# Zero products beside thin matmuls, signs ahead of a sigmoid, and weight loads placed around the decays

## The chip, the cores and the metric

The kernel runs on one core of a Trainium2 chip. The metric is the device time of one execution in microseconds. TensorE is called PE (its weight loads PEld), VectorE DVE, ScalarE ACT, GpSimd POOL, and SyncE, which issues nearly all DMAs, SP.

## The reference

Two things one after the other: a recurrent attention (mLSTM) with exponential gates over 768 steps, for 4 batches and 8 heads of 40, and a bilinear feed-forward on its output, 3072 rows of 320.

```
m_new = max(f + m, i);  f_stab = exp(f + m - m_new);  i_stab = exp(i - m_new)
C = f_stab * C + i_stab * outer(v, k);   n = f_stab * n + i_stab * k
y = sigmoid(o) * (C q) / max(|n q|, 1)
out = ((x @ w_a) * (x @ w_b)) @ w_out        # x is y as rows, 320 -> 1536 -> 320
```

The weights come as float64; the other inputs as float32.

## The kernel before

**Tiling.** The sequence is cut into 6 pieces of 128 steps, and with 4 batches that makes 24 chunks, n = 0 to 23 (piece n // 4, batch n % 4). Inside a chunk the recurrence is a masked, decay-weighted attention; between pieces a state of 40 x 42 per head is carried. Chunks are gathered into 9 moe blocks of 2 or 3 chunks (`sizes`), and `moe_block` multiplies a block's rows with the weights, each value split in a high and a low part.

**Stages of a chunk**, by letter: E builds the decay matrix, A transposes q and k, B makes the scores and weighs them with E, C multiplies with the values, U updates the state, F divides and gates, D transposes the result into the rows of its moe block. Chunks 0 to 5 (`NF32` = 6) take the float32 forms `begin_a`, `begin_b`, `begin_i`, `begin_c`. Chunks 0 to 3 (`NE` = 4) build E on PE (`begin_e`); from chunk 4 on `stage_e` reads the decays back from DRAM, broadcast to all partitions (`load_g`, tile `gbc`, two buffers, freed by the value products of the chunk two before), masks them on POOL (L483) and takes eight exponentials on ACT (L490). `gates_rest` computes these decays on DVE and stores them to `g_dram` (L289).

**Weights.** They come as 32 stages (0 to 31). `fetch(to)` issues the DMAs of all stages below `to` that are not yet issued, on SP. A stage is converted from the words of its float64 in steps: `signs` (ACT, L412), `words` (three DVE instructions, L423 to L426), `leading` (ACT copy, L439), `rests` (two products on PE, L449 and L450, and an addition on DVE, L457, or two halved ones, L455). An up product of the first moe block waits, through `need`, until its stages are converted. The raw tiles of stages 26 to 31 use the room in which q, k and v of chunks 2 and 3 lie.

**Order.** The opening, `start()`, runs inside `in_order()`: every engine gets its instructions in the written order, SP's DMAs too. So does what is left of `gates_rest` behind it. After that the order is the scheduler's: it starts from the order of tracing, by a modelled timeline, and `tc.issue_after(x)` adds that what is traced in its block is queued behind x on x's engine. `attention()` traces the stages of chunk after chunk, with later letters for the next chunk, in between the pieces of the moe blocks.

`busy(count)` issues `count` matmuls of zeros (L959, 336 columns) into a bank that nobody reads; `dense` puts three such ahead of some products of chunks 2 and 3. `weigh` (POOL, L585) scales the values for U with one buffer; `gate_o` is the sigmoid of the output gates (ACT, L217), and the first one in the opening carries a load of ACT's tables.

Of the kernel before, what the change touches and what calls it, by code (L numbers as in the profile page):

```python
# [8 lines left out]
F32 = mybir.dt.float32  # L9
# [5 lines left out]
AF = mybir.ActivationFunctionType  # L15
# [5 lines left out]
def kernel(  # L21
# [13 lines left out]
    nc = tc.nc  # L35
    B, H, S, D = q.shape
    DM, DFF = w_a.shape
    P = 128
# [11 lines left out]
    NF32 = 6  # L50
    NE = 4
# [71 lines left out]
    NS = sizes[0]  # L123
# [90 lines left out]
    def gate_o(c, bs=slice(0, B)):  # L214
        hot[0] = 3
        x = osig[c][:, bs, 0:DM]
        nc.scalar.activation(x, x, AF.Sigmoid)  # L217

    def load_g(n):
        c, b = chunks[n]  # L220
        t = apool.tile([P, H * P], F32, tag="gbc", name=f"gbc{n}")
        t = t.rearrange("p (h t) -> p h t", h=H)
        gbc[n] = t
        return nc.sync.dma_start(t, g_dram[c - 1:c, b * H:(b + 1) * H, :].broadcast_to([P, H, P])).ins
# [150 lines left out]
    def fetch(to):  # L375
        while fetched[0] < min(to, len(stages)):
            x = fetched[0]
            fetched[0] += 1
            src = stages[x]
            n = src[0].shape[1]  # L380
            raw = rpool.tile([P, n], I64, tag=f"s{x}", name=f"raw{x}")
            r0 = 0
            for a in src:
                nc.sync.dma_start(raw[r0:r0 + a.shape[0]], a)
                r0 += a.shape[0]
            held[x] = [raw, n]
# [91 lines left out]
    def stage_e(n):  # L478

        c, b = chunks[n]  # L480
        E = gbc.pop(n)
        st.setdefault(n, {})["E"] = E
        nc.gpsimd.affine_select(  # L483
            E, E, pattern=[[0, H], [1, P]], compare_op=ALU.is_ge, fill=-1e30, base=0,
            channel_multiplier=-1,
        )
        yield
        beta = beta_col(c, b)
        for h in range(H):
            nc.scalar.activation(E[:, h], E[:, h], AF.Exp, bias=beta[:, h:h + 1])  # L490
            if h % 2 == 1:
                yield

# [226 lines left out]
    def attention():  # L720
        for n in range(NS, NCH):
            if NS + 3 < n + 1 < NCH:
                load(n + 1)
            if n == NE:
                fetch(len(stages))
            for o in "BDEACUF":
                if o in "BAC" and n + (o == "A") < NF32:
                    if o == "B":
                        yield from begin_b(n)
                        yield from begin_i(n)  # L730
                    elif o == "C":
                        yield from begin_c(n)
                    else:
                        yield from begin_a(n + 1)
                elif o == "B":
                    yield from stage_b(n, 0)
                    yield from stage_b(n, 1)
                    yield from stage_i(n)
                elif o == "D":
                    if n > NS:  # L740
                        yield from stage_d(n - 1)
                    if n % B == 0 and n > 0:
                        load_o(n // B)
                elif o == "E":
                    if n + 1 < NE:
                        yield from begin_e(n + 1)
                    elif n + 1 < NCH:
                        yield from stage_e(n + 1)
                elif o == "A":
                    if n + 1 < NCH:  # L750
                        yield from stage_a(n + 1)
                        yield from stage_v(n + 1)
                elif o == "U":
                    if NE <= n + 2 < NCH:
                        load_g(n + 2)
                    u = stage_u(n)
                    yield next(u, None)
                    late.append(u)
                    if len(late) > 2:
                        yield from late.pop(0)  # L760
                else:
                    yield from {"C": stage_c, "F": stage_f}[o](n)
        yield from stage_d(NCH - 1)
# [87 lines left out]
    def begin_a(n):  # L851

        T = []
        st.setdefault(n, {})["T"] = T
        if n < NS:
            both = room(f"T{n}").rearrange("p (w h t) -> p w h t", w=2, h=HH)
        for j in range(2):
            if n < NS:
                t = both[:, j]
            else:  # L860
                t = apool.tile([P, 2 * H * P], BF16, tag=f"T{j}", name=f"T{n}_{j}", bufs=1).bitcast(F32)
                t = t[:, 0:HH * P].rearrange("p (h t) -> p h t", h=HH)
            T.append(t)
            if n < NS and n + j > 0:
                pT = ps_dn.tile([P, 512], F32, tag=f"pd{2 * n + j - 1}", name=f"pT{n}_{j}")
            else:
                pT = ps_at.tile([P, 512], F32, tag="pat", name=f"pT{n}_{j}")
            pt = pT.rearrange("p (h t) -> p h t", h=HH)
            for x in range(HH):
                nc.tensor.transpose(  # L870
                    pt[:, x], nat(n)[0][j][:, 2 * x:2 * x + 2, :].rearrange("t h d -> t (h d)"), ident
                )
            (nc.vector.tensor_copy if n >= NS and j == 1 else nc.scalar.copy)(t, pt)
            yield

    def begin_b(n):
# [72 lines left out]
    with tc.tile_pool(name="spool", bufs=3) as spool:  # L949

        def room(name):
            return spool.tile([P, H * P], F32, tag="x", name=name)

        def start():
            warm = ps_dn.tile([P, 512], F32, tag="pd1", name="warm")

            def busy(count):
                for _ in range(count):
                    nc.tensor.matmul(  # L959
                        warm[:, 0:H * DV], zero[:, 0:P], zero, start=True, stop=True  # L960
                    )

            def run(x, count=99):
                for _ in range(count):
                    if next(x, "end") == "end":
                        return

            busy(13)
            f, i = gates_load()
            load_qk(0)  # L970
            load_qk(1)
            fetch(2)
            load_v(0)
            load_v(1)
            fetch(3)
            load_o(0, (0, 1))
            fetch(5)
            load_qk(NS)
            load_o(0, (2, 3))
            fetch(6)  # L980
            load_v(NS)
            fetch(8)
            load(NS + 1)
            fetch(12)
            m0, w = gates_first(f, i)
            rest = gates_rest(f, i, m0)
            a0, e0, b0, e1, b1 = begin_a(0), begin_e(0), begin_b(0), begin_e(1), begin_b(1)
            run(a0, 1)
            busy(2)
            run(a0)  # L990
            busy(2)
            run(b0, 1)
            busy(2)
            run(rest, 1)
            signs(0)
            run(e0)
            words(0)
            run(begin_a(1))
            leading(0)
            signs(1)  # L1000
            run(b0)
            run(e1)
            gates_w(w)
            words(1)
            rests(0)
            run(b1)
            leading(1)
            gate_o(0, slice(0, 2))
            rests(1)
            run(begin_c(0))  # L1010
            weigh(0)
            signs(2)
            run(begin_c(1))
            run(stage_f(0))
            words(2)
            run(stage_u(0))
            load(NS + 2)
            weigh(1)
            leading(2)
            signs(3)  # L1020
            run(stage_f(1))
            d0, d1 = stage_d(0), stage_d(1)
            warm = ps_dn.tile([P, 512], F32, tag="pd2", name="warm2")
            busy(4)
            run(d0, 1)
            words(3)
            run(d0)
            leading(3)
            busy(4)
            rests(2)  # L1030
            signs(4)
            run(stage_u(1))
            fetch(18)
            load(NS + 3)
            fetch(26)
            busy(4)
            run(d1, 1)
            words(4)
            run(d1)
            leading(4)  # L1040
            busy(4)
            rests(3)
            busy(8)
            rests(4)
            signs(5)
            gate_o(0, slice(2, B))
            words(5)
            return rest

        with in_order():  # L1050
            rest = start()
    mpool = ctx.enter_context(tc.tile_pool(name="mpool", bufs=3))
    with in_order():
        for _ in rest:
            pass
    for n in range(max(NS, NE), NS + 2):
        load_g(n)
    def rest():
# [59 lines left out]
```

## Time and profile before

| what | value |
|---|---|
| time, median of 3 runs | 562.77 us (560.14 to 565.24) |
| the profiled execution, its own time | 560.51 us |
| its span in the profile | 558.5 us |
| mean granted clock of PE | 0.993 |
| busy: PE, DVE, ACT, POOL | 544.9, 389.4, 267.9, 126.9 us |
| DMA, moved in all | 66.75 MB, mean 120 GB/s |

The profile is one execution. A row of the timeline gives start and duration in us, the engine, the line in the kernel, the operation, what it writes and reads, its shape and, in brackets, how long the engine was idle before it and for whom it waited; DMA issues stand on SPq or ACTq. A row of a table by stretch gives the stretch and its length, busy time and count of each engine, then the granted clock of PE as a share, the DMA engines' busy share and GB/s. Busy time of PE includes matmuls that wait in its pipeline.

### The profile page before, as it was taken

Reading aid. Unit: us, or ns where it says so; the run is one execution under the profiler, and the core shown is the slowest. Engines: PE = TensorE matmul, PEld = TensorE weight load, DVE = VectorE, ACT = ScalarE, POOL = GpSimd, SP = SyncE. Lnnn points to the kernel's source line nnn. Section 1 sums busy time; section 2 is a strip of 40 time slices with the busy share of each in tenths; the row PEclk is TensorE's granted clock in tenths of the full one; section 3 lists DMA queues with packets and bytes.
Section 4 is the critical chain, followed back from the end, with each engine's and each line's share of the span. In section 5 each row is a group of like instructions: output and inputs, shape, how many; then the busy total and the mean of one; then the engine's idle time right before and its main releaser. Section 6 shows DMA issues by size and latency. Waiting matters only on the chain.

```text
span 558.5 us, 12726 instructions
## 1 busy us (share of the span) xinstructions
PE 544.9 (98%) x4925; PEld 518.0 (93%) x4925; DVE 389.4 (70%) x888; ACT 267.9 (48%) x645; POOL 126.9 (23%) x188
## 2 busy tenths in 40 slices
PE   8999999899999999999999999999999999999997
PEld 6898898799999899999989999998999999999997
DVE  6889999964858683968749774977757755944332
ACT  5574678752626761556525654644526733310111
POOL 3102414641232320332031330333021302000000
PEclk9799999999999999999999999999999999999999
DMA  9999941393649762569536684586539704200001
GB/s 191 215 263 291 290 72 51 94 179 71 108 103 193 141 139 58 123 142 180 107 99 156 108 151 115 118 145 138 118 97 154 144 0 115 48 1 25 0 1 35
DMA packets 198551, 66.75 MB, mean 120 GB/s; under 512 B 184220, under 2 KB 191772, under 8 KB 198492
## 3 DMA queue, kind: packets, MB, share of 16 engines
q1 hardware_dynamic: 198444, 65.86, 56.4%
q8 instruction: 38, 0.62, 0.5%
q14 instruction: 21, 0.17, 0.1%
q10 hardware_dynamic: 48, 0.10, 0.0%
HBM read 41.11 MB, written 5.95 MB: 84 GB/s over the span
## 4 chain that ended last, share of the span: by engine, by line
PE 60%; DMA 17%; DVE 10%; ACT 5%; issue 3%; SPq 3%; POOL 1%; ACTq 0%; DVEq 0%; POOLq 0%
PE pu L810 31%; PE pd L781 15%; DMA T<-qks 4%; DMA c_dram<-cb 3%; ACT gbc L490 3%; DMA va<-in_v_dram 2%; PE pV L603 2%; PE pU L628 2%; DVE gbc L554 2%; DMA gbc<-g_dram 1%; DMA raw<-in_moe_w_a_dram 1%; DVE pb L556 1%; PE pS L884 1%; PE pV L927 1%; PE pS L545 1%
## 5 line engine op out<-in xcount | busy, mean ns | idle before, releaser
L810 PE MATMUL pu<-xh,w 128*128 128x384 f32 (+1 forms) x1080 | 276.5, 324 | 2.6 <-ACT g L816 0.9
L810 PE MATMUL pu<-xl,w 128*128 128x384 f32 (+1 forms) x648 | 208.0, 322 | 0.0
L810 PEld LDWEIGHTS pu<-xh,w 128*128 128x128 f32 x1080 | 190.6, 189 | 5.9 <-ACT g L816 1.3
L781 PE MATMUL pd<-w,gh 128*128 128x320 f32 x576 | 126.7, 309 | 0.0
L810 PEld LDWEIGHTS pu<-xl,w 128*128 128x128 f32 x648 | 122.2, 189 | 0.2
L817 DVE TENSOR_TENSOR g<-pu,g 128x384 f32<-128x384 f32 (+1 forms) x108 | 54.6, 505 | 89.4 <-PE pu L810 46.3
L781 PEld LDWEIGHTS pd<-w,gh 128*128 128x128 f32 x576 | 96.7, 188 | 0.1
L781 PE MATMUL pd<-w,gl 128*128 128x320 f32 x288 | 85.3, 310 | 0.0
L816 ACT COPY g<-pu 128x384 f32<-128x384 f32 (+1 forms) x90 | 39.6, 440 | 93.4 <-PE pu L810 84.2
L490 ACT ACTIVATE gbc<-gbc,gtab 128x128 f32<-128x128 f32 x160 | 49.1, 389 | 18.1 <-POOL gbc L483 18.0
L821 DVE TENSOR_TENSOR gl<-g,gh 128x384 fp32r<-128x384 f32 (+1 forms) x92 | 52.2, 568 | 1.9
L781 PEld LDWEIGHTS pd<-w,gl 128*128 128x128 f32 x288 | 53.1, 188 | 0.2
L585 POOL TENSOR_TENSOR vw<-va,gtab 128x336 f32<-128x336 f32 x20 | 16.4, 822 | 160.3 <-PE pU L628 135.2
L819 DVE CAST gh<-g 128x384 fp32r<-128x384 f32 (+1 forms) x108 | 41.1, 382 | 2.2
L483 POOL TENSOR_SCALAR_AFFINE_SELECT gbc<-gbc 128x1024 f32<-128x1024 f32 x20 | 22.6, 1132 | 65.1 <-DMA gbc<-g_dram 32.9
L554 DVE TENSOR_TENSOR gbc<-gbc,pb 128x512 f32<-128x512 f32 x36 | 27.2, 757 | 6.8 <-ACT pb L552 6.6
L603 PEld LDWEIGHTS <-pb 128*128 128x128 bf16 x576 | 23.4, 96 | 6.4 <-DVE pb L556 3.2
L684 POOL TENSOR_TENSOR osig<-osig,den 128x320 f32<-128x320 f32 x22 | 16.6, 754 | 54.9 <-DVE den L671 42.9
L603 PE MATMUL pV<-va,pb 128*128 128x42 bf16 x288 | 25.9, 183 | 2.7 <-DVE pb L556 2.7
L790 ACT COPY o<-pd 128x320 f32<-128x320 f32 x24 | 8.8, 434 | 40.3 <-PE pd L781 40.3
L550 DVE TENSOR_TENSOR gbc<-pS,gbc 128x512 f32<-128x512 f32 x36 | 23.7, 682 | 4.0 <-PE pS L545 4.0
L518 ACT COPY qks<-qks 128x640 bf16<-128x640 bf16 x36 | 26.0, 725 | 0.6
(154 smaller groups left out, 849.6 us busy)
## 6 DMA issues: line engine op xcount, KB each, us to landing
gbc<-g_dram SPq DMA_DIRECT2D x20, 512.0 KB
q<-in_q_dram SPq DMA_DIRECT2D x24, 160.0 KB
k<-in_k_dram SPq DMA_DIRECT2D x24, 160.0 KB
va<-in_v_dram SPq DMA_DIRECT2D x24, 160.0 KB
osig<-in_o_gate_dram SPq DMA_DIRECT2D x24, 160.0 KB
raw<-in_moe_w_out_dram SPq DMA_DIRECT2D x12, 320.0 KB
out_dram<-o SPq DMA_DIRECT2D x24, 160.0 KB
raw<-in_moe_w_a_dram SPq DMA_DIRECT2D x8, 384.0 KB
```

The lines of the kernel that those rows point to most:

```text
L483: nc.gpsimd.affine_select(E, E, pattern=[[0, H], [1, P]], compare_op=ALU.is_ge, fill=-1e30, base=0, channel_multiplier=-1,)
L490: nc.scalar.activation(E[:, h], E[:, h], AF.Exp, bias=beta[:, h:h + 1])
L518: nc.scalar.copy(qks[:, 0, :, lo:lo + 2 * D], qks[:, 1, :, D - lo:3 * D - lo])
L550: nc.vector.tensor_tensor(E, pS, E, op=ALU.mult)
L554: nc.vector.tensor_tensor(E, E, pb[:, 0], op=ALU.subtract)
L603: nc.tensor.matmul(pv[:, h], pb[i][:, h % HH, :], vb[j][:, h], start=(x == 0), stop=(x == len(terms) - 1),)
L781: nc.tensor.matmul(pd[t][:, 0:DM], a[:, cols], w, start=(ff == 0 and first), stop=(ff == NF - 1 and last),)
L810: nc.tensor.matmul(acc[j], a, r, start=(x == 0), stop=(x == len(terms) - 1),)
L816: (nc.vector.tensor_copy if ff in [1, 2] else nc.scalar.copy)(g, acc[0])
L817: nc.vector.tensor_tensor(g, acc[1], g, op=ALU.mult)
L819: nc.vector.tensor_copy(gh, g)
L821: (nc.gpsimd if kb * 12 + ff < 16 else nc.vector).tensor_tensor(gl, g, gh.bitcast(F32), op=ALU.subtract)
```

## The change

Four edits:

1. In the opening, the zero products move. Two come ahead of the value products of chunk 0 (`begin_c(0)`), four between those of chunks 0 and 1, three behind chunk 0's division; of those that stood behind (4, 4, 4, 4 and 8) two groups of four are left. The stages around them are put in another order: the transposes of chunk 0 (`d0`) come ahead of its state product (`stage_u(0)`), `weigh(1)` with them.
2. `signs(2)` comes ahead of the first `gate_o`, and `fetch(3)` goes, so that stage 2 is fetched behind the first output gates.
3. `fetch(26)` leaves the opening. Stages 18 to 21 are fetched behind the rest of the gates, which ends with the decays; 22 to 25 behind chunk 4's read of the decays, and 26 to 31 behind chunk 5's, in place of a fetch at the head of chunk 4.
4. For chunks 4 and 5, A is traced ahead of E, and E's exponentials are queued on ACT behind the last ACT copy of a chunk's transposes (`after["t"]`).

```
@@ stage_e
-            nc.scalar.activation(E[:, h], E[:, h], AF.Exp, bias=beta[:, h:h + 1])
+            with tc.issue_after(after["t"]) if n < NF32 else nullcontext():
+                nc.scalar.activation(E[:, h], E[:, h], AF.Exp, bias=beta[:, h:h + 1])
@@ attention
-            if n == NE:
-                fetch(len(stages))
-            for o in "BDEACUF":
+            for o in "BDAECUF" if NE <= n + 1 < NF32 else "BDEACUF":
...
-                        load_g(n + 2)
+                        with tc.issue_after(load_g(n + 2)):
+                            fetch(26 if n == NS else len(stages))
@@ begin_a
-            (nc.vector.tensor_copy if n >= NS and j == 1 else nc.scalar.copy)(t, pt)
+            if n >= NS and j == 1:
+                nc.vector.tensor_copy(t, pt)
+            else:
+                after["t"] = nc.scalar.copy(t, pt).ins
@@ start
-            fetch(3)
             load_o(0, (0, 1))
             fetch(5)
...
             run(b1)
+            warm = ps_dn.tile([P, 512], F32, tag="pd2", name="warm2")
             leading(1)
+            signs(2)
             gate_o(0, slice(0, 2))
             rests(1)
+            busy(2)
             run(begin_c(0))
             weigh(0)
-            signs(2)
+            busy(4)
             run(begin_c(1))
             run(stage_f(0))
+            busy(3)
             words(2)
+            d0, d1 = stage_d(0), stage_d(1)
+            run(d0, 1)
+            leading(2)
+            signs(3)
+            weigh(1)
+            run(stage_f(1))
+            run(d0)
+            rests(2)
+            words(3)
+            leading(3)
+            signs(4)
             run(stage_u(0))
             load(NS + 2)
-            weigh(1)
-            leading(2)
-            signs(3)
-            run(stage_f(1))
-            d0, d1 = stage_d(0), stage_d(1)
-            warm = ps_dn.tile([P, 512], F32, tag="pd2", name="warm2")
             busy(4)
-            run(d0, 1)
-            words(3)
-            run(d0)
-            leading(3)
-            busy(4)
-            rests(2)
-            signs(4)
+            run(d1, 1)
+            rests(3)
+            words(4)
+            run(d1)
+            leading(4)
             run(stage_u(1))
             fetch(18)
             load(NS + 3)
-            fetch(26)
             busy(4)
-            run(d1, 1)
-            words(4)
-            run(d1)
-            leading(4)
-            busy(4)
-            rests(3)
-            busy(8)
             rests(4)
             signs(5)
@@ behind start
     with in_order():
         for _ in rest:
             pass
+        fetch(22)
```

## The prediction

> **What bounds the kernel now.** I read the page first, then the sums by stretch, then the first 110 us engine by engine.
>
> ```profile
> span 558.5 us, 12726 instructions
> PE 544.9 (98%) x4925; PEld 518.0 (93%) x4925; DVE 389.4 (70%) x888; ACT 267.9 (48%) x645; POOL 126.9 (23%) x188
> 15.00:30.00 15.00, 15.00 (x111) 12.69 (x112) 11.09 (x28) 8.94 (x19) 1.71 (x2) 0.77 1.18 217
> 30.00:110.00 80.00, 77.81 (x636) 70.02 (x635) 78.05 (x194) 55.23 (x138) 27.01 (x37) 1.00 0.68 175
> ```
>
> The columns of the last two rows are the stretch, its length, then busy time (with instructions) of PE, PEld, DVE, ACT and POOL, the granted clock, DMA share and GB/s. Over the whole span PE looks like the bound. The change, however, edits only the code for the first stretches, and there the picture differs: from 30 to 110 us DVE is busy 78.05 of 80 us, and PE gets 636 matmuls, 8.0 a microsecond, where the whole span has 4925, 8.8 a microsecond. That is the stretch in which the weights are converted (words, rests) beside chunks 2 to 5. Its length is DVE's work, so what can be won is mainly how early DVE gets into it. From 15 to 30 us DVE is idle for 3.9 us, and the granted clock is 0.77.
>
> ```profile
> 15.37 3.90 PE L927 MATMUL pV<-va,gbc 128*128 128x42 f32 x32
> 19.20 1.54 PE L628 MATMUL pU<-vw,k 128*64 128x42 f32 x16
> 20.67 1.30 PE L959 MATMUL warm<-zero 128*128 128x336 bf16 x4
> 27.50 1.31 PE L959 MATMUL warm<-zero 128*128 128x336 bf16 x8
> 53.29 0.92 PE L628 MATMUL pU<-vw,k 128*64 128x42 f32 x16
> 15.23:18.64 3.41, 3.41 (x33) 1.00 0.89 198
> 18.65:22.06 3.41, 3.41 (x26) 0.50 1.53 158
> 22.06:25.47 3.41, 3.41 (x24) 0.50 1.07 294
> ```
>
> The last three rows are windows of PE alone: length, PE busy (count), clock. After a window that holds almost nothing but the value products of chunks 0 and 1 (42 columns each), the clock is 0.50 for two windows, 6.8 us, and a group of 16 state products takes 1.54 us there against 0.92 at full clock. Four zero products take 1.30 us, eight at full clock 1.31.
>
> **The change part by part.** In the opening, every engine runs in written order, so I follow DVE's row.
>
> ```profile
> 17.29 0.17 DVE L669 TENSOR_SCALAR den<-pV 128x8 f32<-128x8 f32 x1 [0.36 <-PE pV L927]
> 18.91 0.35 DVE L423 TENSOR_SCALAR cw<-qks 128x384 uint32<-128x384 uint32 x1
> 20.17 0.16 DVE L669 TENSOR_SCALAR den<-pV 128x8 f32<-128x8 f32 x1
> 21.98 0.36 DVE L423 TENSOR_SCALAR cw<-qks 128x384 uint32<-128x384 uint32 x1
> 24.41 0.56 DVE L457 TENSOR_TENSOR w<-pc,cw 128x384 fp32r<-128x384 f32 x1 [0.62 <-PE pc L450]
> 24.89 0.35 DVE L423 TENSOR_SCALAR cw<-qks 128x384 uint32<-128x384 uint32 x1
> 27.28 0.56 DVE L712 TENSOR_TENSOR xl<-pX,xh 128x384 fp32r<-128x384 f32 x1 [1.06 <-ACT xh L711]
> 27.76 0.55 DVE L457 TENSOR_TENSOR w<-pc,cw 128x384 fp32r<-128x384 f32 x1
> 29.64 1.14 DVE L455 TENSOR_TENSOR w<-pc,cw 64x384 fp32r<-64x384 f32 x2 [1.33 <-PE pc L450]
> 16.11 1.28 ACT L217 ACT_TABLE_LOAD   x1 [1.83 <-DMA osig<-in_o_gate_dram]
> ```
>
> *Zero products and the order of the opening.* DVE's steps from these starts: stage_f(0) 18.91-17.29 = 1.62; words(2) 20.17-18.91 = 1.26; stage_f(1) 21.98-20.17 = 1.81; one xl 27.76-27.28 = 0.48; one rests 24.89-24.41 = 0.48; the last, halved rests about 1.17 (two adds of 1.14 us together). With three words, two xl and two rests before the last, the work is 1.62 + 1.81 + 3 x 1.26 + 2 x 0.48 + 2 x 0.48 + 1.17 = 10.3 us. Before, it begins at 17.29 and ends at 30.8; the three bracketed waits of 0.62, 1.06 and 1.33 us (3.0 together) are waits for PE, the second by way of ACT; PE at half clock works through 4, 4, 4, 4 and 8 zero products ahead of the product that DVE needs.
>
> Afterwards 2 + 4 + 3 stand around the values of chunks 0 and 1 and 4 + 4 later: 17 instead of 24. Price of one at full clock, 1.31/8 = 0.16 (the row's end includes drain; taken as is). The first two push the first den by 0.3, to 17.6; the other seven lie on PE while DVE does stage_f(0) and words(2), 2.9 us against 1.2 of zeros, so they are hidden. Of the 24 that stood around pU and pX, eight remain, each four behind a product that DVE already has. So 17.6 + 10.3 = 27.9, if nothing were waited for. What is late next: the first xl now comes behind stage_f(1), because its copy on ACT is queued behind that stage's column copy (an estimate: 0.6, as for the product at 24.41); the products of rests(3) and rests(4) can only start when the words just ahead on DVE end, 0.4 to 0.5 each, an estimate from the same row. Together 1.5: the opening ends near 29.4, **1.4 us earlier**. The bounds: 2.9 earlier (no waits), 0.6 earlier (half clock again in PE's work of 25 to 29 us, at which a pU costs 1.54 - 0.92 = 0.6 more, and the rests products an estimated 0.2).
>
> On this place the Trainium skill ("TensorE: Matmul & The Clock Gate", section "HAM oscillation — how this bites in real kernels") says that the clock falls when the engine idles for over about 3.4 us between bursts. The trace does not bear that out as it stands: the window 15.23 to 18.64 has PE busy for 3.41 of 3.41 us and the clock fell behind it. By that rule the zero products would buy no clock, and the new gap of 2.4 us would cost none: 561.0 again, without the rival of the moved half clock.
>
> By the rows, thin products count like idling. The longest new stretch without a product is about 22.8 to 25.2 us, from the second transpose to the end of words(3), worked out with the steps above; it could cost the clock.
>
> *Signs ahead of the sigmoid.* signs(2) fills ACT's 1.83 us wait for the output gates. But its weights are now fetched behind those gates, so both land by about 16.1, where the gates land now: signs(2) starts there, and the table load and the sigmoid come about 0.5 us later. stage_f(0), itself 0.3 later, uses the sigmoid only in its last product. I cost it at zero; without that cover it is 0.2, and nothing is won, since words(2) is queued behind stage_f(0) on DVE anyway.
>
> *Weight stages and decays.*
>
> ```profile
> 38.23 1.66 DVE L283 TENSOR_TENSOR_SCAN gates_m<-one,g_f 32x128 f32<-32x128 f32 x5
> 45.41 0.76 SPq L384 DMA_DIRECT2D raw<-in_moe_w_a_dram  x1
> 52.69 0.34 SPq L289 DMA_DIRECT2D g_dram<-gates_m  x1
> 54.89 0.58 ACT L873 COPY T<-pT 128x512 f32<-128x512 f32 x1 [0.19 <-PE pT L870]
> 59.30 0.33 SPq L224 DMA_DIRECT2D gbc<-g_dram  x1
> 65.99 1.09 POOL L483 TENSOR_SCALAR_AFFINE_SELECT gbc<-gbc 128x1024 f32<-128x1024 f32 x1 [0.94 <-DMA gbc<-g_dram]
> 67.60 2.44 ACT L490 ACTIVATE gbc<-gbc,gtab 128x128 f32<-128x128 f32 x8
> 66.13 0.39 PE L810 MATMUL pu<-xh,w 128*128 128x256 f32 x1 [0.40 <-DVE g L817]
> ```
>
> The decays are scanned by 39.9 us, but their store goes out at 52.69, because stages 18 to 25 (from 45.41) stand ahead of it on SP. With only stages up to 17 ahead it goes out near 45; stages 18 to 21 follow it, and chunk 4's read of the decays near 50 instead of 59.30. Stages 22 to 25 stand behind that read, 26 to 31 behind chunk 5's. Chunk 4's mask and exponentials then come some 8 to 9 us earlier (65.99 and 67.60 now). The exponentials are queued behind the copy of that chunk's transposes, which ACT does at 54.89 now, so that edit holds nothing back. What is this worth? Nothing of it is DVE work removed, and DVE has 1.95 us of idling from 30 to 110. PE's gap of 0.40 at 66.13 may go: I take **0.4**, between -6.3 and +8.5 (the rivals below).
>
> Sum: 1.4 + 0.4 = 1.8 us. The profiled execution took 560.51 us (2.0 around its span), so 558.7; it lies 2.26 under the median of 562.77, so on that scale **561.0**.
>
> **The rivals.**
>
> *Half clock moves (little or no gain).* The new stretch of about 2.4 us without products sets the clock to 0.50 from about 25.5 on. For: the row of 15.23, which fell while PE was never idle. Against: in the row from 30 to 110 the clock is 1.00 through many small products. Price 0.8 in the opening, and PE's first moe products at half rate in what is left of 6.8 us, about 1: 562.8.
>
> *Chunks 4 and 5 run ahead (faster).* POOL's and DVE's attention work now crowds the end of the conversion.
>
> ```profile
> 40.88 1.18 POOL L821 TENSOR_TENSOR gl<-g,gh 128x256 fp32r<-128x256 f32 x1 [0.89 <-DVE gh L819]
> 41.40 1.07 DVE L426 SCALAR_TENSOR_TENSOR cr<-raw,qks 128x384 fp32r<-128x384 uint32 x1
> 102.33 1.05 DVE L670 TENSOR_TENSOR den<-num,den 128x8 f32<-128x8 f32 x1
> 100.00:110.00 10.00, 8.25 (x56) 6.98 (x55) 9.65 (x22) 8.22 (x24) 7.22 (x13) 1.00 0.32 69
> ```
>
> Beside POOL's 1.18 us one, a product that else takes 0.56 takes 1.07; the small den product takes 1.05 at 102.33, where POOL is busy for 7.22 of 10 us with 13 operations. If these spread out, some nine stretched DVE operations at 0.5 us each, an estimate from these rows, come back: 561.0 - 4.5 = 556.5. The Trainium skill ("SBUF — State Buffer", "Who interferes with whom") makes such a pair block each other wholly; the 1.07 agrees. Against: the same POOL operations have to run somewhere beside DVE, which has no room before.
>
> *Weights behind waits (slower).*
>
> ```profile
> SPq L224 <- PE pV L927: 16.3, 2, 13.8
> 66.23 0.33 ACT L646 CAST cb<-cst 128x168 bf16<-128x168 f32 x1 [2.04 <-DMA c_dram<-cb]
> 60.00:70.00 10.00, 9.60 (x79) 8.63 (x78) 9.88 (x25) 6.43 (x20) 4.44 (x5) 1.00 0.96 257
> gbc<-g_dram SPq DMA_DIRECT2D x20, 512.0 KB
> raw<-in_moe_w_out_dram SPq DMA_DIRECT2D x12, 320.0 KB
> raw<-in_moe_w_a_dram SPq DMA_DIRECT2D x8, 384.0 KB
> ```
>
> SP runs in order, and its read of the decays waits for the value products that free the buffer (16.3 us in two waits, the longer one for a later chunk). Stages 26 to 31 now stand behind chunk 5's read, which needs chunk 3's products. They (three of w_a and w_b at 384 KB, three of w_out at 320) and the read are 2,624 KB; at the 257 GB/s of this stretch 10.5 us. If the stores of the state's parts (c_dram) are put behind them, ACT's cast, which waits 2.04 for such a store already, waits 10.5, and with it the signs that feed DVE: 8.5 more, 569.5. It decides from the point where ACT's wait exceeds what DVE has in hand, a stage or two of words (2.5 us). Against: the stores may be placed ahead of the stages, as most of them are now, and the raw stages are converted much later than they land.
>
> *It does not do what it says.* The schedule behind the opening is remade and eats the 1.4 us: DVE's stretch has the same work in another order, and PE's later stalls fall differently, 1 us to either side: 562.
>
> **How the numbers follow.** Forecast 0.47 (own range 559 to 563.5), half clock moves 0.15, no effect 0.08, chunks ahead 0.19, weights behind waits 0.11. Single runs of before lie from 560.14 to 565.24, so a median of three can be off by over 1 us; 1%, 5.6 us, is about what a measurement tells from no change. The faster rival reaches below 557.1 in most of its mass, and a little of the forecast does with it: 0.20. The slower one lies over 568.4 in most of its mass: 0.10. Within: 0.70. The range 555.5 to 566.5 leaves out the slower rival and little on the fast side.
>
> **What would show it.** Right: no 0.50 clock between 18 and 26 us, the two adds of rests(4) near 28 to 28.5 (29.64 now), the decays' store near 45, chunk 4's exponentials before 62, and DVE still above 9.5 of 10 us up to about 105. Half clock moves: 0.50 in a window from 25 us on. Chunks ahead: POOL's operations of 100 to 110 spread over 70 to 100 and the last L457 well before 105. Weights behind waits: waits of ACT for c_dram, or of ACT's signs for raw data, of over 4 us between 60 and 80. I am wrong if the change is over 1% either way for a reason in PE's stretch after 150 us, which I take as untouched, or if before's median run has a worse opening than the profiled one.

## The result, and the profile after

| | before | after |
|---|---|---|
| median, in the same series | 562.09 us (558.75 to 565.62, 20 runs) | 564.92 us (562.15 to 568.83, 20 runs) |
| ratio of after to before | | 1.0061, 95% interval 1.0042 to 1.0080 |
| profiled execution, span | 558.5 us | 563.3 us |

The change makes the kernel 0.6% slower; 561.0 us, a gain of 1.8 us, had been forecast. All ratios are to runs of before in the same series on the same chip (medians of 559.53 us for e1 to e5, 560.46 for e7 to e10, 559.50 for e11 to e13 and e15, 560.71 for e14, e16 and e17). The ratios and their intervals leave out executions over 1.5% above the fastest of their kernel, so they do not follow exactly from the medians given.

First the stretches of the profile after, read as those of before (stretch, length, busy time and count of PE, PEld, DVE, ACT and POOL, clock, DMA share, GB/s):

```profile
span 563.3 us, 12703 instructions
15.00:30.00 15.00, 12.52 (x102) 9.85 (x102) 11.30 (x30) 8.68 (x19) 1.75 (x2) 0.89 1.05 194
30.00:110.00 80.00, 75.56 (x600) 67.66 (x597) 72.64 (x179) 50.88 (x123) 22.79 (x29) 0.98 0.68 174
50.00:60.00 10.00, 8.40 (x70) 6.82 (x69) 6.92 (x19) 4.74 (x13) 3.07 (x5) 1.00 0.93 318
60.00:70.00 10.00, 10.00 (x79) 9.13 (x78) 8.70 (x23) 7.80 (x23) 2.95 (x4) 0.83 0.37 66
```

The loss is in the conversion: from 30 to 110 us DVE works 72.64 us where it worked 78.05. It has the same 888 instructions in both kernels, so 5.4 us of its work are pushed behind 110 us; the span is 4.8 longer. This goes together in all seventeen profiles of this document: DVE's busy time from 15 to 110 us and the span add up to between 643.6 and 649.3 us, while the span alone goes from 555.5 to 574.1. Most of the loss falls between 50 and 70 us. The row of before for the first half of that place, and its value weights (vw) and rounding (cr) on POOL:

```profile
50.00:60.00 10.00, 10.00 (x93) 8.68 (x92) 9.13 (x23) 7.33 (x21) 2.79 (x4) 1.00 1.04 354
57.46 0.75 POOL L585 TENSOR_TENSOR vw<-va,gtab 128x336 f32<-128x336 f32 x1 [2.36 <-ACT w L439]
58.16 0.58 POOL L647 TENSOR_TENSOR cr<-cst,cb 128x168 f32<-128x168 f32 x1
```

The timeline after the change, by engine (issues on SPq):

```profile
45.30 2.07 SPq L289 DMA_DIRECT2D g_dram<-gates_m  x1
50.30 0.33 SPq L224 DMA_DIRECT2D gbc<-g_dram  x1
57.01 1.09 POOL L483 TENSOR_SCALAR_AFFINE_SELECT gbc<-gbc 128x1024 f32<-128x1024 f32 x1 [6.49 <-PE pX L708]
58.07 0.75 POOL L586 TENSOR_TENSOR vw<-va,gtab 128x336 f32<-128x336 f32 x1
58.77 0.50 POOL L648 TENSOR_TENSOR cr<-cst,cb 128x168 f32<-128x168 f32 x1
58.87 0.66 PE L629 MATMUL pU<-vw,k 128*64 128x42 f32 x10 [1.60 <-POOL vw L586]
59.31 0.33 DVE L636 TENSOR_TENSOR cst<-cst,dec 128x168 f32<-128x168 f32 x1 [2.60 <-POOL cr L648]
59.31 0.33 ACT L651 CAST cb<-cr 128x168 bf16<-128x168 f32 x1 [3.76 <-POOL cr L648]
62.94 0.59 ACT L876 COPY T<-pT 128x512 f32<-128x512 f32 x1
63.42 2.45 ACT L491 ACTIVATE gbc<-gbc,gtab 128x128 f32<-128x128 f32 x8
```

The decays' store and read are early, as forecast (45.30 and 50.30). But chunk 4's mask now stands on POOL ahead of chunk 3's value weights (vw) and the rounding of chunk 2's state (cr); before, it stood behind both (vw at 57.46, mask at 65.99). The mask starts 6.7 us after its read was issued. Behind it wait PE, DVE and ACT. (The mask's idle time is put down to a product long done; other runs below name the read.)

The opening, in the same form:

```profile
16.72 0.55 ACT L412 ACTIVATE qks<-raw 128x384 f32<-128x384 f32 x1 [2.58 <-DMA raw<-in_moe_w_a_dram]
18.58 0.74 ACT L217 ACTIVATE osig<-osig 128x640 f32<-128x640 f32 x1
19.35 0.49 DVE L681 TENSOR_TENSOR osig<-y,osig 128x320 f32<-128x320 f32 x1 [0.78 <-ACT osig L217]
26.34 0.56 DVE L457 TENSOR_TENSOR w<-pc,cw 128x384 fp32r<-128x384 f32 x1 [0.71 <-PE pc L450]
29.68 1.14 DVE L455 TENSOR_TENSOR w<-pc,cw 64x384 fp32r<-64x384 f32 x2 [0.24 <-PE pc L450]
22.80:26.20 3.40, 1.57 (x9) 1.00 1.02 319
26.20:29.60 3.40, 3.40 (x24) 0.50 1.42 173
```

The last two rows are windows of PE alone (length, PE busy with count, clock, DMA share, GB/s): busy for 1.57 of 3.40 us, and behind that 3.4 us of half clock. The adds of rests(4) are at 29.68, where they were at 29.64, though most of words(5) now stands ahead of them.

### The profile page after: what moved, and what is told of

It reads as the page before. It is cut to its first block, busy times and chain, and to the rows that moved or that the text cites. A ratio compares the mean times of both kernels' runs of the same rounds, so it can differ in the third digit from the quotient of the medians.

```text
span 563.3 us, 12703 instructions
## 1 busy us (share of the span) xinstructions
PE 545.0 (97%) x4918; PEld 517.9 (92%) x4918; DVE 388.8 (69%) x888; ACT 268.9 (48%) x645; POOL 126.6 (22%) x188
## 4 chain that ended last, share of the span: by engine, by line
PE 64%; DVE 11%; DMA 10%; SPq 5%; ACT 4%; issue 3%; POOL 2%; ACTq 0%; DVEq 0%; POOLq 0%
PE pu L810 34%; PE pd L781 17%; DMA gbc<-g_dram 3%; ACT gbc L491 3%; PE pV L604 3%; PE pU L629 2%; DMA va<-in_v_dram 2%; SPq L207 2%; DVE gbc L555 2%; PE pS L546 2%; DMA c_dram<-cb 1%; DMA T<-qks 1%; DVE pb L557 1%; DMA q<-in_q_dram 1%; SPq L384 1%
## 5 line engine op out<-in xcount | busy, mean ns | idle before, releaser
L513 DVE TENSOR_TENSOR r<-k,qks 128x320 f32<-128x320 f32 x18 | 9.5, 528 | 24.5 <-ACT qks L509 24.5
```

## The experiments

Each group names its run as its expectation does.

**Which part loses?** The opening alone (its order, zero products and signs, with the old fetches), and the moved weight stages alone:

```
e1:  start() of the change in the kernel before, with fetch(26) kept
e2:  -  fetch(26) in start, -  if n == NE: fetch(len(stages))
     +  fetch(22) behind the gates, +  with tc.issue_after(load_g(n + 2)): fetch(...)
```

> The kernel before with the new opening alone (zero products, order, signs ahead of the sigmoid, stage 2 fetched behind the gates); the fetches of stages 18 to 31 and chunk 4's and 5's order stay as before. Theory A (the mask of chunk 4 stands on POOL ahead of other work and waits for a read that the fetch edit lets the schedule count on too early): the opening has no part in the loss, so 1 us faster to 0.5 us slower than before. Theory B (half clock moved to 26 us and the sigmoid is later: the opening itself loses): 2 to 3 us slower. Theory C (weights 22 to 31 land too late): same as A here.

> The kernel before with the fetch edit alone: 18 to 21 behind the decays' store, 22 to 25 behind chunk 4's read, 26 to 31 behind chunk 5's. A: the loss is here, 2.5 to 5 us slower than before, with POOL's mask of chunk 4 waiting for its read at about 55 to 58 us and ACT, DVE and PE waiting behind POOL for 1.5 to 4 us. B: within 1 us of before. C: 2 to 5 us slower too, but with waits of ACT's signs for raw data and none behind POOL.

Measured: 567.75 us, ratio 1.0132 (1.0098 to 1.0166) for the opening, 566.06 us, 1.0091 (1.0053 to 1.0128) for the stages. Both parts lose alone, the opening clearly more than both together (the interval of the stages overlaps with that of the change); my theory that the stages carry all of it fell. The profile of the opening alone:

```profile
60.00:70.00 10.00, 5.44 (x46) 5.07 (x45) 3.61 (x9) 3.62 (x11) 1.81 (x2) 0.96 0.76 207
65.26 1.09 POOL L483 TENSOR_SCALAR_AFFINE_SELECT gbc<-gbc 128x1024 f32<-128x1024 f32 x1 [8.16 <-DMA gbc<-g_dram]
66.38 1.86 ACT L490 ACTIVATE gbc<-gbc,gtab 128x128 f32<-128x128 f32 x6 [6.91 <-POOL gbc L483]
70.14 0.36 DVE L423 TENSOR_SCALAR cw<-qks 128x384 uint32<-128x384 uint32 x1 [6.35 <-ACT qks L412]
```

Nothing near 60 us was edited there. Yet chunk 4's exponentials now stand on ACT ahead of the signs that DVE needs (and of a copy of transposes), and the mask ahead of a vw on POOL; all of them wait for the decays, which land near 65 as before. The scheduler has made the order behind the opening anew.

Two runs on the fetches inside the change: the read of the decays ahead of all of stages 18 to 25, and the old fetches with the new opening and chunk 4's new order.

```
e4:  -        fetch(22)                       # behind the gates
e5:  the change with the fetches of before
```

> The changed kernel, but stages 18 to 21 are fetched behind chunk 4's read as well, so that the read stands right behind the decays' store. POOL's order stays that of the change. A: the read lands near 51 to 53 us, POOL's mask waits for nothing that others need, and 3 to 4 us of the loss go: within 1 us of before. B: as slow as the change, 3 us over before. C: weights land still later, so slower than the change, 4 to 6 us over before.

> The changed kernel with the fetches of before (all of 18 to 25 in the opening, 26 to 31 at the head of chunk 4): opening and chunk order are new. A: the mask stands behind the scaled values and the state's remainder on POOL again, no wait there, and the time is within 1 us of before. B: 2 to 3 us slower than before. C: as A.

```profile
53.79 1.09 POOL L483 TENSOR_SCALAR_AFFINE_SELECT gbc<-gbc 128x1024 f32<-128x1024 f32 x1 [2.60 <-DMA gbc<-g_dram]
50.00:60.00 10.00, 10.00 (x83) 8.11 (x82) 9.89 (x24) 6.45 (x18) 4.03 (x5) 1.00 0.94 293
70.00:80.00 10.00, 10.00 (x59) 9.11 (x58) 8.00 (x20) 3.47 (x8) 2.81 (x3) 0.83 0.69 210
```

Measured: 564.34, ratio 1.0073 (1.0044 to 1.0102), and 569.77, 1.0192 (1.0142 to 1.0242). Of e5:

```profile
62.97 1.19 POOL L483 TENSOR_SCALAR_AFFINE_SELECT gbc<-gbc 128x1024 f32<-128x1024 f32 x1 [6.02 <-DMA gbc<-g_dram]
```

The first rows are of e4: with the read first, the mask starts 4.3 us after it (issued at 49.5), DVE is full from 50 to 60, and yet the total does not move; time is missing from 70 to 80 instead, in a window of half clock. On DVE, ACT and POOL every instruction of e4 stands in the order of the change, so the stall went without a gain. In e5 the order differs from the change in the mask alone, which stands behind vw and cr again; but it waits for a read that is late again, and the next vw stands behind it. (The profile of e5 is its slowest execution, 574.96 us.) So one wait less is not one gain more. What the order itself costs takes runs that hold it.

**The opening against the order behind it.** A helper gives each engine's instructions behind `start()` an ordering edge to the one ahead of them in a list taken from another kernel's final order:

```
+    mark = len(nc.cur_bb.bb.instructions)      # behind rest = start()
...
+    held_order(tc, nc, mark)                   # behind the last moe block
```

> The new opening alone, and behind it every engine's instructions held in the order in which they stood before (the new opening alone, with an order made anew behind it, was 1.3% slower than before). If the order made anew is what costs (the opening itself starts the first expert products 1.5 to 2 us earlier): 557 to 559 where before is 559.5, a ratio of 0.995 to 1.000, and DVE busy over 9.5 of 10 us from 40 to 80 us. If the new opening costs by itself (its zero products, its late signs, its transfers): 565 to 568, a ratio over 1.009.

> The opening of before, and behind it every engine's instructions held in the order that was made anew behind the new opening. If that order is what costs: 567 to 570, a ratio of 1.013 to 1.019, with DVE idle for several us between 55 and 75 us. If the new opening costs by itself: 558 to 561, as before.

| | order of before | order made anew behind the new opening |
|---|---|---|
| old opening | 1 (before) | e10: 567.57 us, 1.0127 (1.0097 to 1.0156) |
| new opening | e9: 561.47 us, 1.0021 (0.9999 to 1.0044) | e1: 1.0132 (1.0098 to 1.0166) |

The columns differ by 1.1 to 1.3%, the rows by at most 0.2%. The order that the scheduler makes behind the new opening alone costs; between these two orders the opening neither gains nor loses much. In e10 (its line numbers, like those of all held runs, are higher by 67):

```profile
60.00:70.00 10.00, 2.50 (x22) 2.18 (x20) 1.01 (x3) 2.82 (x10) 1.81 (x2) 0.74 0.77 199
66.06 1.09 POOL L550 TENSOR_SCALAR_AFFINE_SELECT gbc<-gbc 128x1024 f32<-128x1024 f32 x1 [11.41 <-DMA gbc<-g_dram]
67.18 1.86 ACT L557 ACTIVATE gbc<-gbc,gtab 128x128 f32<-128x128 f32 x6 [10.93 <-POOL gbc L550]
```

Its first expert product starts at 26.8 us, 2.9 earlier than in e1 (29.7), and ACT waits 4.0 us longer for the same landing: in these two executions, what the opening is ahead is only waited off. That fits with rows that do not differ.

**The wait on POOL.** The change without its opening, and the whole change with chunk 4's mask behind cr:

```
e8:  edits 3 and 4 of the change on the kernel before
e7:  +                    elif n + 1 == NE:
     +                        weigh(n)
     +                        yield from late.pop(0)      # cb of chunk 2
     +                        with tc.issue_after(after["cb"]):
     +                            mask_e(n + 1)
```

> The change without its opening: the weight stages moved behind the reads of the decays, chunk 4's order and its exponentials behind the copy of the transposes. Chunk 4's mask stands on POOL ahead of the value weights of chunk 3 and of the rounding of a state, as after the whole change. If waiting there for the read of the decays is what costs: 562 to 566, and POOL's mask waits over 4 us while PE waits for POOL's value weights. If the opening is what costs: 557 to 560.

> The whole change, with chunk 4's mask put behind chunk 3's value weights and chunk 2's state rounding on POOL; up to 110 us nothing else is moved on any engine. If the mask's wait for the decays is what costs: the waits of PE, ACT and DVE for POOL at 57 to 59 us go, DVE is busy over 9 of 10 us from 50 to 60 (6.9 after the change) and the time falls by 2 to 3 us, to 561.5 to 563 where the change has 564.9 and before 559.5. If the opening costs by itself, or something else late in the conversion: within 1 us of the change, 564 to 566.

Measured: e8 1.0055 (1.0013 to 1.0097), its executions spread from 559.93 to 576.39 us; e7 563.17 us, 1.0043 (1.0020 to 1.0067). Rows of POOL in e8, then in e7, whose line numbers differ:

```profile
55.27 1.09 POOL L483 TENSOR_SCALAR_AFFINE_SELECT gbc<-gbc 128x1024 f32<-128x1024 f32 x1 [9.55 <-DMA gbc<-g_dram]
```

```profile
55.60 0.58 POOL L653 TENSOR_TENSOR cr<-cst,cb 128x168 f32<-128x168 f32 x1
57.09 1.18 POOL L480 TENSOR_SCALAR_AFFINE_SELECT gbc<-gbc 128x1024 f32<-128x1024 f32 x1
50.00:60.00 10.00, 10.00 (x83) 8.11 (x82) 9.87 (x24) 6.45 (x18) 3.66 (x5) 1.00 0.93 316
```

In e7 the mask runs at the same time as after the change, but ahead of it cr is done at 55.60 instead of 58.77, and DVE is full from 50 to 60. From 30 to 110 us DVE gets back 3.5 of its 5.4 us (76.14). In the times about 1 us comes back, less than the 2 to 3 expected; the intervals of e7 and of the change overlap, so the stall is shown, its price only roughly. The profiled execution of e8 has the stall too (DVE works 7.51 of 10 us from 50 to 60) and took 560.46 us, the median of before. Part of the loss is elsewhere: from 60 to 90 us DVE does less than before even where the stall is gone (rows of before, e7 and e4), and no run isolates why:

```profile
60.00:90.00 30.00, 29.60 (x238) 26.98 (x237) 29.45 (x75) 23.29 (x58) 9.04 (x11) 1.00 0.62 143
60.00:90.00 30.00, 30.00 (x241) 27.44 (x240) 27.40 (x71) 21.66 (x53) 6.80 (x8) 1.00 0.69 164
60.00:90.00 30.00, 30.00 (x230) 27.51 (x228) 25.54 (x67) 20.20 (x51) 6.21 (x7) 0.94 0.77 180
```

**The opening by itself**, all in the order of before behind it. In the new opening, signs(2) put back behind the sigmoid with its fetch; the nine zero products alone in the old opening; the new opening without them:

```
e11: -            signs(2)                    +  fetch(3) ahead of load_o(0, (0, 1))
     +            signs(2)                    # behind weigh(0)
e12: +  busy(2), busy(4), busy(3) around begin_c(0), begin_c(1), in the kernel before
e13: -  busy(2), busy(4), busy(3) of the new opening
```

> The new opening with the order of before held behind it, and in it signs(2) put back behind the sigmoid and its stage fetched ahead of the output gates again; one instruction of ACT and one transfer change places, nothing else. If signs(2) ahead of the sigmoid costs (it starts at 16.7 to 17.4, when its weights land, and the sigmoid is late for DVE by 0.8 to 1.2 us): that wait of DVE goes, the adds of rests(4) come 0.8 to 1.2 us earlier, and the time is 0.5 to 1.2 us under the held opening's, 560.3 to 561 where before has 560.5. If what DVE has then is only waited for later: the adds of rests(4) stay near 30, and 561.5.

> Before, with the nine zero products around the values of chunks 0 and 1 alone (2, 4 and 3) and the 24 others kept, the order behind the opening held. If they hold the clock: no 0.50 between 18 and 28 us, the adds of rests(4) near 27 to 28 (29.6 in the profiled run of before, which has 6.8 us of 0.50; 27.0 in a run of that opening without it) and a time of 558.5 to 560, below before's. If the clock drops whether or not they are there: 0.50 somewhere from 18 to 30 us, or none in before either, and 560 to 561, as before.

> The new opening without its nine zero products around the values, the order of before held behind it. If they hold the clock there: 0.50 from about 18 us on, as in the profiled run of before, and a time 1 to 2 us over the held opening with them, 562.5 to 563.5. If they do nothing: 561 to 561.8, and the half clock, where it comes, comes late, from 22 to 27 us, as with them.

Measured: e11 560.17 us, 1.0002 (0.9971 to 1.0032); e12 558.59, **0.9975** (0.9952 to 0.9998); e13 560.84, 1.0024 (0.9995 to 1.0054). First rows of e11, then one window of PE in e13, then e12:

```profile
26.12 0.56 DVE L524 TENSOR_TENSOR w<-pc,cw 128x384 fp32r<-128x384 f32 x1 [1.10 <-PE pc L517]
29.46 1.14 DVE L522 TENSOR_TENSOR w<-pc,cw 64x384 fp32r<-64x384 f32 x2 [0.59 <-PE pc L517]
21.70:25.10 3.40, 1.56 (x15) 1.00 1.04 289
25.10:30.00 4.90, 4.90 (x29) 0.50 1.29 229
```

```profile
18.50:22.00 3.50, 2.34 (x11) 0.53 0.74 97
```

```profile
15.00:30.00 15.00, 15.00 (x142) 12.80 (x142) 13.17 (x32) 10.27 (x22) 1.59 (x2) 1.00 1.16 220
27.67 1.14 DVE L522 TENSOR_TENSOR w<-pc,cw 64x384 fp32r<-64x384 f32 x2 [0.52 <-PE pc L517]
```

The nine do what they are for: in the old opening with them the clock is 1.00 throughout, and the adds of rests(4) are at 27.67. One profile alone would not show it, but over all executions the mean granted clock is 0.998 in e12 and 0.994 in before. In e11 the wait of DVE for the sigmoid is gone, but a half clock from 25.1 takes it back in waits for PE. e13 took as long as e9: in its profile (its slowest execution, 566.22 us), without the nine, the half clock comes early (0.53), with them late.

**Why late, and does it add up?** Twelve zero products put back into e11's opening; the change with both e7's mask and e11's signs; and e7's order behind the old opening, without and with the nine zero products:

```
e17: +            busy(4)     # ahead of rests(3) (behind run(d1, 1)), of stage_u(1) and of rests(4)
e14: the edits of e7 and e11 on the change, in e7's order
e15: the opening of before with e7's order behind it (edits 3 and 4, mask moved)
e16: e15 with the nine zero products of e12
```

> The new opening with signs(2) behind the sigmoid (held order, 1.0002 of before), and twelve zero products more, in three fours where PE waited for DVE: ahead of chunk 1's state products, of its second part of stage_d and of the last rests. If the missing zero products bring the half clock from 22 to 27 us: none before 30 us, the adds of rests(4) near 28.5 (29.5 without them), and a ratio of 0.996 to 0.999. If the clock drops for another reason, or the zero products stand in the way of the products behind them: 0.50 in some window from 22 us, or the adds at 29.5 or later, and a ratio of 1.000 to 1.003.

> The whole change with signs(2) and its stage put back behind the sigmoid and ahead of the output gates, and chunk 4's mask behind chunk 3's value weights and chunk 2's state rounding on POOL; every other instruction in the order of the run with the mask moved. If these two carry the loss: as before, a ratio of 1.000 to 1.003 (the change 1.006, with the mask moved 1.004). If a third cause is left in the order behind the opening: 1.004 to 1.006.

> The change without its opening, with chunk 4's mask behind chunk 3's value weights and chunk 2's state rounding on POOL, every engine held in the order that this gave behind the new opening (there 563.2, against 564.9 with the mask ahead). If the weight stages behind the reads of the decays and chunk 4's order are worth what was forecast once POOL waits for nothing: 559.5 to 560.5, at or just under before (560.5). If the order that they bring costs by itself: 562 to 564, and DVE idle for 2 us or more between 60 and 80 us, as in the run with the new opening.

> The old opening with the nine zero products added (by itself 0.9975), and behind it the rest of the change with the mask moved (by itself 1.0011). If the two add up: 0.997 to 1.000. If the earlier opening is lost again in the order behind it: 1.001 to 1.004.

Measured: e17 558.86 us, **0.9967** (0.9942 to 0.9992); e14 562.43, 1.0031 (1.0005 to 1.0056); e15 560.35, 1.0011 (0.9986 to 1.0036); e16 558.28, 0.9975 (0.9950 to 1.0000). e17:

```profile
15.00:30.00 15.00, 13.71 (x119) 10.93 (x120) 11.92 (x30) 9.12 (x20) 1.78 (x2) 1.00 1.19 218
28.84 1.14 DVE L522 TENSOR_TENSOR w<-pc,cw 64x384 fp32r<-64x384 f32 x2 [0.29 <-PE pc L517]
```

With twelve more zero products there is no half clock in the opening (nor in e12 and e16, which have more still), and the kernel is faster than before and than the change. Over all executions the mean granted clock is 0.997 in e17 and 0.994 in e11. So the late half clock most likely came with the zero products that the change took away; the times of e17 and e11 have intervals that overlap. e16 lies under e15 by 0.36%, as e12 under before by 0.25%: as far as the intervals tell, the nine add up with the rest of the change. That rest, once POOL does not wait, is worth nothing that can be measured (e15). e14 is between what I gave: the two repairs together do not bring the whole change back to before; its profile has half clock at 25 us, as e11, and again between 66 and 83, where from 60 to 80 us DVE works 15.2 of 20. What brings on those later ones I did not settle.

Behind the opening, e7, e14, e15 and e16 have one order on DVE, ACT and POOL, so they can be read as a chain: 1.0061 for the change, 1.0043 with the mask moved, 1.0011 with the old opening in place of the new, 0.9975 with the nine zero products in it. By these values the mask costs 0.2%, the new opening 0.3%, the rest of edits 3 and 4 0.1%; the intervals of the first three overlap, so the shares are rough.

## Why the prediction was wrong

The forecast was the sum of two gains, 1.4 us in the opening and 0.4 us from the decays. Both steps failed. By the chain of runs above, and as roughly, the new opening costs 0.3%, 1.8 us, and the mask's place on POOL 0.2%, 1 us.

- **"The opening ends near 29.4, 1.4 us earlier": failed.** Against the profiled before 0.7 came: the adds start at the same time, but two of three instructions of words(5), 0.41 and 0.33 us, stand ahead of them.

  *The waits for PE* were sized well: 0.69, 0.71 and 0.24 us, 1.6 for the forecast 1.5. *"Signs ahead of the sigmoid: zero"* is the term that was missing: the weights landed at 16.72 instead of 16.1, the sigmoid began 1.2 us later (18.58 against 17.41), and DVE waited 0.78, in e1 1.19. e11 takes that wait away; in the times 1.0021 (e9, where the wait was only 0.17) against 1.0002 is within the intervals. Half clock, the reason named for the lower bound of 0.6, came, but it is not what held the adds: e1 has full clock throughout its opening and waits as long for PE.

  *The starting point* was wrong as well: the profiled before had 6.8 us of half clock in its opening. With the same opening at full clock, in e10, DVE waits 0.7 us in all, and the adds are at 27.01 (27.99 in e15, also at full clock). The rows of e1, then that of e10:

```profile
23.99 0.56 DVE L712 TENSOR_TENSOR xl<-pX,xh 128x384 fp32r<-128x384 f32 x1 [0.69 <-ACT xh L711]
26.98 0.56 DVE L457 TENSOR_TENSOR w<-pc,cw 128x384 fp32r<-128x384 f32 x1 [0.71 <-PE pc L450]
30.31 1.14 DVE L455 TENSOR_TENSOR w<-pc,cw 64x384 fp32r<-64x384 f32 x2
27.01 1.14 DVE L522 TENSOR_TENSOR w<-pc,cw 64x384 fp32r<-64x384 f32 x2 [0.40 <-PE pc L517]
```

From the first den (17.67 in e1, 17.69 in e10) to the adds, with 0.7 us of words(5) taken off in e1, the new order takes 2.6 us more than the old one at the same clock: it waits for the sigmoid and for PE where the old order does not. The forecast gain was one over an execution at half clock, not over the old order. Which opening is usual in before is open: its executions have a mean clock of 0.993 to 0.994, which tells of half clock, but not where. A reading was wrong too: of before's five groups of zero products only the first two ran at half clock; from 25.5 us on it was full again.

  *"Of the 24, eight remain, each behind a product that DVE already has":* true, but the sixteen that went had kept PE busy, and their loss was counted as pure gain; with twelve put back, the adds of e17 are 0.62 us ahead of those of e11.
- **"Half clock moves", the rival at 0.15: its mechanism came.** It put the cause at 22.8 to 25.2 us and the fall near 25.5; the fall was at 26.2, behind a window from 22.8 to 26.2 that is 1.57 of 3.40 us busy, and it came in seven of eight profiled executions of the new opening with its 17 zero products, between 22 and 27.1 us. Its price of 0.8 us in the opening did not: DVE waits 0.24 us at the adds there. I gave it too small a chance because the row from 30 to 110 us has many small products at full clock; that row has PE busy for 77.81 of 80 us, which this window has not.
- **"Chunk 4: 0.4 earlier": failed at its cover.** Store and read came when forecast, the mask 9.0 us earlier. But I took the order on POOL as given and priced the move of the mask by DVE's and PE's gaps alone, not by what is queued behind it: 1.60, 2.60 and 3.76 us on three engines. And "that edit holds nothing back" was wrong: the copy of transposes is itself at 62.94 now (54.89 before), so the exponentials came at 63.42, not before 62, though the mask was done at 58.1. The bounds of this term also mix two bases: -6.3 counts from before, +8.5 from the forecast.
- **"It does not do what it says": right in kind, wrong in size.** "The schedule behind the opening is remade" is what happened. I wrote 1 us to either side; the order that the new opening alone brings lost 1.27%, 7 us, behind the old opening (e10). The order of the whole change is another one: with the mask moved it loses 0.11% there (e15).
- **"Weights behind waits": not as told.** In the list of waits of the changed kernel from 50 to 80 us neither ACT nor DVE waits for c_dram or for raw data. The slower side came by an in-order queue, as there, but by POOL's (in the change) and ACT's (in e1).
- **"Chunks 4 and 5 run ahead": no.** DVE was to stay over 9.5 of 10 us; it fell to 6.92 from 50 to 60, where before had 9.13.

On the clock, the windows of 3.4 us ahead of the falls have PE busy for 1.57 (after), 1.56 (e11), 1.94 (e9) and 2.38 us (e4), and PE's longest gap in the opening of the change is 1.17 us. The busy share alone does not decide: in e1 a window of 1.57 us brought no fall, and e17 kept full clock through one of 2.13.

```profile
23.00:26.40 3.40, 1.57 (x13) 1.00 1.12 324
22.00:25.40 3.40, 2.13 (x14) 1.00 1.01 288
```

The Trainium skill ("TensorE: Matmul & The Clock Gate", "HAM oscillation — how this bites in real kernels") asks for idle gaps over about 3.4 us; in the opening of the change the clock fell with gaps of at most 1.17 us. The same page of the Trainium skill, "A second HAM failure mode: psum-queue depth-cycling", says that frequent short idling between groups of matmuls makes the clock oscillate too; seven of the eight openings agree with that, e1 does not.

## What to carry to other kernels

An instruction that waits for a transfer is priced by what is queued behind it on its engine, and an edit early in a scheduled kernel moves such instructions far from the edit: compare each engine's order before and after, and measure the edit with the later order held, or the two effects cannot be told apart. Moving such an instruction's transfer earlier does not help if the schedule moves the instruction further. Compare a change with several executions of before: a profile whose clock happened to fall makes the old order look slower than it is. Zero products are worth counting over windows of 3.4 us, the length of one half-clock stretch here: where they went and PE was left with 1.6 to 2.4 us of work in such a window, the clock mostly fell.

## What the runs showed of the hardware

- A window of thin products (42 columns) with PE busy for 3.40 to 3.41 us is followed by half clock in three of six executions without the nine zero products around it (before, e8, e13; not in e2, e10, e15), and with them in none of eleven. One profile does not tell the state of such a stretch.
- A read of 512 KB (the decays, broadcast) was usable 6.4 to 6.7 us after its issue where a weight stage had been issued within 2.1 us ahead of it (before 59.30 to 65.99, after 50.30 to 57.01, e8 48.83 to 55.27), and 4.0 to 4.3 us after where none had for 3.9 us or more (e1, e4, e5). That the stages are the reason is not shown.
- A stall of the engines around PE can be followed by half clock: in e10 PE has no product for 8.0 us up to 70.5, and the clock is at half from 64.9 to 75.1.
